# Splitting w1's conversion into three slices, moving g's columns to their own PSUM bank, and holding back two later loads

## The chip, the cores and the metric

The kernel runs on one NeuronCore of one Trainium2 chip. The metric is the device time of one execution in microseconds (us), lower is better. The core's engines are called PE (TensorE, matrix products), DVE (VectorE), ACT (ScalarE), POOL (GpSimd) and SP (SyncE, which here only issues DMAs). "PEld" stands for PE's weight loads.

## What is computed

x is float32 of 8 x 4224 x 192. A causal convolution of seven taps runs along the sequence, with one softmax-normalised set of taps for each of 8 heads of 24 channels. Its result goes through a layer norm (with gain g), two matrix products with a ReLU between them, and a residual sum:

```python
w = np.exp(weight - np.max(weight, axis=-1, keepdims=True))
w = w / (np.sum(w, axis=-1, keepdims=True) + 1e-09)          # weight: 8 heads x 7 taps
x_unf = x_pad[:, idx, :].reshape(B, S, K, H, group)          # K = 7, H = 8, group = 24
x = np.einsum('hk,bskhg->bshg', w, x_unf).reshape(B, S, D)   # D = 192
mu = np.mean(x, axis=-1, keepdims=True)
var = np.mean((x - mu) ** 2, axis=-1, keepdims=True)
xn = (x - mu) / np.sqrt(var + 1e-06) * g_ln
ch = np.maximum(xn @ w_ch1, 0.0) @ w_ch2                     # 192x768 and 768x192
return (x + ch).astype(np.float32)
```

The two matrices arrive as float64. The kernel reads them as pairs of 32-bit words and builds float32 from the bits itself.

## The kernel before

**Groups.** The sequence is cut into groups of rows, each laid over 128 partitions: group 0 has 6 rows for each partition, group 1 has 8 (the rows left over, from all eight batches), group 2 has 10, and from group 3 on there are 16. The main loop (L967) goes through the groups: `up` or `up_mixed` makes the hidden layer on PE, `down` or `down_fast` brings it back to 192 channels, and between them the convolution, transpose and statistics of the next groups are worked on by DVE and ACT. The schedule is manual: every engine runs its instructions in the order in which the program writes them, and the framework puts in the semaphores.

**The start**, which is all that the change touches, has these pieces.

- *Small inputs* (L195 to L209). ACT issues three small DMAs: the weights of the taps (L197) and g in two pieces (L199, L200). PE spreads the weights over all partitions with a matmul against a row of ones (L203), and turns g into two columns with two matmuls against ones (L205). All three write the bank `spread`. L268 to L277 make the normalised `taps` on DVE, with the exponential on ACT (L272); `gs` is the copy of g's columns (L273).
- *Loads on SP* (L211 to L224): w1's first 128 rows in one transfer into `raw1[:, 0:2]` (L211), the other 64 rows as two transfers into `raw1[:, 2]` (L215), group 0's x (`load_x(0)`: partitions 16 to 127, then 1 to 15 (L164), then the first (L171)), group 1's x (`load_x(1)`: eight transfers of 16 partitions each, L139), and w2's words (L221).
- *Words to float32*. `split_words` (L231) issues three DVE instructions (L233, L235, L239) and two on ACT (L234, L242); `join_words` (L244) issues three on DVE (L247, L250, L258 with g, or L256 without). w1 goes through in two pieces, of 768 columns (`words_a`) and of 384 (`words_b`), into `w1f`; w2 in one of 1152 columns later (L952 to L955).
- *Tap matrices*. For heads 5, 6 and 7 (`PE_HEADS`) the convolution of group 0 runs on PE, against diagonal matrices that hold the taps. `tap_matrices` (L324) writes those of heads 5 and 6 on ACT (L327), three taps before and four after w1's first split. POOL builds those of head 7 (L319).
- *Warm-up*. `keep_warm(20)` (L943) issues 20 matmuls of constants that POOL filled (`less`, L306, and `copy`); each shows as two passes, so as 40 instructions at L376.
- *Group 0's convolution.* `first_tap` (ACT, L397) starts `y` for heads 0 to 4, `conv` (DVE, L422) adds the other six taps, `transpose` (DVE, L433) prepares `yt` for PE.
- *`centre_w1`* (L340) takes the column means out of w1 on PE. In order: the mean's products over `w1f`'s slices 0 and 1 (L343), the convolution of one head (L334), the products over slice 2 (L346) with their copies (L347), a second head, then for slices 0, 2 and 1 the products L358 and L363 into four banks each and four copies on ACT (L368) into `w1`. The third head comes after slice 0.
- *The main stream*. `up(0)` (L544) takes sets of four PSUM banks, multiplies `yt` with `w1` (L538), and each set is evicted by ACT with a ReLU (L528).

PSUM has eight banks. `take_bank` (L119) deals them out in turn, `take_set` (L124) rounds up to the next multiple of four.

## Time and profile before

| what | value |
|---|---|
| median of 3 runs | 964.65 us (964.38 to 965.06) |
| profiled execution | 964.9 us, of which the span is 963.2 us |
| PE busy | 951.7 us (99%) |
| DVE busy | 894.1 us (93%) |
| ACT busy | 683.9 us (71%) |
| POOL busy | 252.8 us (26%) |
| DMA | 166.69 MB, mean 173 GB/s |
| first L538 (main stream on PE) | 27.31 us after the span's start |

The span is the time from the first to the last record of the profiled execution; all times of single instructions count from its start. Busy times overlap between engines. A busy PE is not a PE at its peak. In a line of a timeline the first number is the start, the second how long it lasts; then come engine, program line, operation, what it writes and reads, and in square brackets how long the engine idled before it and what ended that idle time. A chain of waits goes back from the last instruction, always to what released it.

### The profile page before, as it was taken

Reading aid. Unit: us, or ns where it says so; the run is one execution under the profiler, and the core shown is the slowest. Engines: PE = TensorE matmul, PEld = TensorE weight load, DVE = VectorE, ACT = ScalarE, POOL = GpSimd, SP = SyncE. Lnnn points to the kernel's source line nnn. Section 1 sums busy time; section 2 is a strip of 40 time slices with the busy share of each in tenths; the row PEclk is TensorE's granted clock in tenths of the full one; section 3 lists DMA queues with packets and bytes.
Section 4 is the critical chain, followed back from the end, with each engine's and each line's share of the span. In section 5 each row is a group of like instructions: output and inputs, shape, how many; then the busy total and the mean of one; then the engine's idle time right before and its main releaser. Section 6 shows DMA issues by size and latency. Waiting matters only on the chain.

```text
span 963.2 us, 38407 instructions
## 1 busy us (share of the span) xinstructions
PE 951.7 (99%) x17280; PEld 717.3 (74%) x17280; DVE 894.1 (93%) x1503; ACT 683.9 (71%) x1101; POOL 252.8 (26%) x386
## 2 busy tenths in 40 slices
PE   7999999999999999999999999999999999999997
PEld 6886586776858677686968778695867868586787
DVE  6999998999999999999999999999999899999757
ACT  5724669587787959687795968779695877867451
POOL 2004411612125131432116131341215221161400
PEclk9999999999999999999999999999999999999999
DMA  9343787769788796969788796978779696777241
GB/s 191 107 125 133 156 213 183 192 125 282 142 241 162 201 201 125 275 134 256 144 232 165 170 246 121 276 139 237 158 180 228 118 282 135 180 136 127 52 85 68
DMA packets 26234, 166.69 MB, mean 173 GB/s; under 512 B 3157, under 2 KB 4054, under 8 KB 18263
## 3 DMA queue, kind: packets, MB, share of 16 engines
q0 software_dynamic: 19552, 100.93, 54.4%
q1 hardware_dynamic: 6512, 63.31, 18.0%
q8 instruction: 135, 2.21, 0.9%
q14 instruction: 29, 0.24, 0.1%
q10 hardware_dynamic: 6, 0.00, 0.0%
HBM read 38.93 MB, written 50.33 MB: 93 GB/s over the span
## 4 chain that ended last, share of the span: by engine, by line
PE 95%; DMA 2%; POOL 1%; ACT 1%; DVE 1%; issue 0%; ACTq 0%; POOLq 0%; DVEq 0%
PE ps L538 46%; PE ps L816 41%; PE ps L763 6%; DMA room<-parts_cs 1%; PE ps L376 1%; DMA room<-in_moe_g_ln_dram 1%; PE ps L334 1%; DVE room L783 0%; DMA out_dram<-y 0%; ACT room L634 0%; DMA room<-room 0%; ACT room L647 0%; POOL d L465 0%; PE ps L358 0%; POOL room L601 0%
## 5 line engine op out<-in xcount | busy, mean ns | idle before, releaser
L422 DVE SCALAR_TENSOR_TENSOR y<-xg,taps,y 128x384 f32<-128x384 f32 (+3 forms) x734 | 367.2, 577 | 0.2
L538 PE MATMUL ps<-yt,w 32*128 32x256 f32 (+2 forms) x4104 | 236.2, 379 | 0.2 <-ACT room L528 0.2
L816 PE MATMUL ps<-room,w2sums 128*32 128x256 f32 (+1 forms) x4320 | 236.2, 375 | 0.1
L634 ACT COPY room<-ps 128x1024 f32<-128x1024 f32 (+1 forms) x135 | 175.0, 1297 | 78.2 <-PE ps L538 77.9
L538 PEld LDWEIGHTS ps<-yt,w 32*128 32x128 f32 x4104 | 204.7, 185 | 26.6 <-issue 9.3
L816 PEld LDWEIGHTS ps<-room,w2sums 128*32 128x32 f32 x4320 | 137.6, 110 | 93.4 <-ACT room L647 5.5
L816 PE MATMUL ps<-room,w 128*32 128x256 f32 (+1 forms) x3240 | 180.7, 375 | 0.3 <-ACT room L647 0.2
L783 DVE TENSOR_TENSOR room<-room 128x1024 f32<-128x1024 f32 (+1 forms) x135 | 151.0, 1192 | 6.4 <-PE ps L816 6.4
L816 PEld LDWEIGHTS ps<-room,w 128*32 128x32 f32 x3240 | 103.8, 110 | 69.4 <-DVE room L640 5.0
L538 PE MATMUL ps<-ysums,w1sums 32*128 32x256 f32 x2160 | 124.9, 379 | 0.0
L538 PEld LDWEIGHTS ps<-ysums,w1sums 32*128 32x128 f32 x2160 | 108.7, 185 | 11.2 <-ACT room L634 3.6
L822 ACT COPY cs<-ps 128x256 f32<-128x256 f32 (+1 forms) x180 | 66.5, 372 | 42.6 <-PE ps L816 42.6
L647 ACT ACTIVATE room<-room 128x1024 f32<-128x1024 f32 (+1 forms) x74 | 90.7, 1250 | 7.3 <-DMA room<-parts_cs 7.1
L894 ACT ACTIVATE ot<-ot,r 128x192 f32<-128x192 f32 x232 | 94.0, 464 | 0.0
L901 POOL DMA_DIRECT2D out_dram<-ot x40 | 34.3, 1084 | 196.9 <-ACT ot L894 121.5
L397 ACT ACTIVATE y<-xg,taps 128x384 f32<-128x384 f32 (+3 forms) x141 | 72.6, 607 | 6.5 <-DVE st L453 6.5
L640 DVE TENSOR_TENSOR room<-room,ps 128x2048 f32<-128x2048 f32 x17 | 38.9, 2288 | 39.4 <-PE ps L538 37.1
L453 DVE BATCH_NORM_STATS2 st<-y 128x6 f32<-128x192 f32 x264 | 70.2, 344 | 0.0
L538 PE MATMUL ps<-yt,w1sums 32*128 32x256 f32 x1080 | 65.2, 380 | 0.0
L822 ACT COPY room<-ps 128x256 f32<-128x256 f32 (+1 forms) x90 | 33.6, 374 | 43.9 <-PE ps L816 35.0
L538 PE MATMUL ps<-ysums,w 32*128 32x256 f32 x1080 | 64.5, 376 | 0.0
L408 ACT ACTIVATE tb<-xg,taps 128x384 f32<-128x384 f32 x112 | 61.9, 636 | 0.0
(109 smaller groups left out, 888.2 us busy)
## 6 DMA issues: line engine op xcount, KB each, us to landing
xg<-in_x_dram SPq DMA_DIRECT2D x15, 2112.0 KB, 18.1
room<-room POOLq DMA_DIRECT2D x45, 512.0 KB, 5.3
out_dram<-ot POOLq DMA_DIRECT2D x29, 768.0 KB, 8.5
y<-tb POOLq DMA_DIRECT2D x28, 768.0 KB, 10.4
out_dram<-y SPq DMA_DIRECT2D x13, 1536.0 KB, 9.4
room<-parts_cs POOLq DMA_DIRECT2D x14, 1024.0 KB, 7.8
room<-parts_tb POOLq DMA_DIRECT2D x14, 1024.0 KB, 7.6
xg<-in_x_dram SPq DMA_DIRECT2D x1, 1536.0 KB
```

Source lines behind the costliest of these rows:

```text
L397: nc.scalar.mul(y[g][:, 0:n, cs], xg[g][:, 0:n, cs], taps[:, h, 0:1])
L408: nc.scalar.mul(tb[g][:, 0:n, cs], xg[g][:, 1 : 1 + n, cs], taps[:, h, 1:2])
L422: nc.vector.scalar_tensor_tensor(out=y[g][:, 0:n, cs], in0=t[:, k : k + n, cs], scalar=taps[:, h, k : k + 1], in1=y[g][:, 0:n, cs], op0=AL ...
L453: nc.vector.bn_stats(out=sums[g][:, j, :], in_=y[g][:, j, :])
L538: nc.tensor.matmul(banks[:, q, i * w : i * w + w], right[rows, c, P * i : P * i + P], left[rows, :, c, :], start=(first and c == 0 and i = ...
L634: nc.scalar.activation(dst, src, AF.Relu) if relu else nc.scalar.copy(dst, src)
L647: nc.scalar.activation(c, c, AF.Relu)
L763: nc.tensor.matmul(bank[C * q : C * q + C, 0:w], w2[:, f, C * c : C * c + C], left, start=(f == 0), stop=(f == NF - 1),)
L783: nc.vector.tensor_tensor(a[:, *dst, f], a[:, *left, f], a[:, *right, f], op=op)
L816: nc.tensor.matmul(dst[C * q : C * q + C, 0:w], right[:, f, C * c : C * c + C], left[:, f, q], start=(first and f == PAIR), stop=(f == PAI ...
L822: nc.scalar.copy(to[:, c], dst[:, 0:w].rearrange("p (j t) -> p j t", t=t))
L894: nc.scalar.mul(ots[g][:, j, :], ots[g][:, j, :], rstd[g][:, j : j + 1])
```

## The change

w1's first 128 rows come in two transfers, one for each slice of 384 columns. w1 is converted in three slices of 384 columns, the split of one slice ahead of the join of the slice before. g's two matmuls go to a bank of their own, after six of the warm-up matmuls; four more come after them, and `keep_warm(20)` goes. `gs` is copied on ACT after the first slice's split. `tap_matrices` writes the seven matrices of one head at a time, head 5 after the join of slice 0 and head 6 after that of slice 1. The heads on PE go in the order 7, 5, 6. The loads of w2's words and of group 1's x are issued after a one-element memset of w2's tile on DVE, which comes after the join of slice 1; w2's words are now ahead of group 1's x.

```diff
-    for r in range(2):
-        nc.tensor.matmul(
-            spread[:, H * K + r : H * K + r + 1], g_row[:, P * r : P * r + P], ones[:, 0:1],
-            start=True, stop=True,
+    raw_taps = spread[:, 0 : H * K].rearrange("p (h k) -> p h k", k=K)
+
+    for s in range(2):
+        nc.sync.dma_start(
+            out=raw1[:, s].rearrange("p f w -> p (f w)"),
+            in_=w1_words[0:P, 2 * FH * s : 2 * FH * (s + 1)],
         )
-    raw_taps = spread[:, 0 : H * K].rearrange("p (h k) -> p h k", k=K)
-
-    nc.sync.dma_start(
-        out=raw1[:, 0:2].rearrange("p s f w -> p (s f w)"), in_=w1_words[0:P, :]
-    )
     for r in range(2):
         nc.sync.dma_start(
             out=raw1[Q * r : Q * r + Q, 2, :, :].rearrange("p f w -> p (f w)"),
             in_=w1_words[P:D, 2 * FH * r : 2 * FH * (r + 1)],
         )
     load_x(0)
-    load_x(1)
-    nc.sync.dma_start(
-        out=raw2.rearrange("p (c d) w -> p c (d w)", d=D),
-        in_=w2_words.rearrange("(c p) d -> p c d", p=P),
-    )
...
-    raw1a = raw1[:, 0:2].rearrange("p s f w -> p (s f) w")
-    raw1b = raw1[:, 2]
...
     nc.scalar.activation(taps, taps, AF.Exp)
-    nc.scalar.copy(gs, spread[:, H * K : H * K + 2])
...
-    words_a = (raw1a, carve(2 * FH, I32), carve(2 * FH, I32))
-    words_b = (raw1b, carve(FH, I32), carve(FH, I32))
+    words_1 = [(raw1[:, s], carve(FH, I32), carve(FH, I32)) for s in range(3)]
...
-    def tap_matrices(ks):
-        for k in ks:
-            for i, h in enumerate(PE_HEADS[:-1]):
-                nc.scalar.mul(diag[:, i, k, :], unit, taps[:, h, k : k + 1])
+    def tap_matrices(h):
+        for k in range(K):
+            nc.scalar.mul(diag[:, h - PE_HEADS[0], k, :], unit, taps[:, h, k : k + 1])
...
-        conv_on_pe(PE_HEADS[0])
+        conv_on_pe(PE_HEADS[2])
         for r in range(2):
             nc.tensor.matmul(pm[r], share[1 + r], w1f[:, 2, :], start=False, stop=True)
             nc.scalar.copy(mean[:, FH * r : FH * r + FH], pm[r])
-        conv_on_pe(PE_HEADS[1])
+        conv_on_pe(PE_HEADS[0])
...
             if s == 0:
-                conv_on_pe(PE_HEADS[2])
+                conv_on_pe(PE_HEADS[1])
...
-    tap_matrices(range(3))
-    split_words(*words_a)
-    tap_matrices(range(3, K))
-    join_words(w1f[:, 0:2].rearrange("p s f -> p (s f)"), *words_a, ga)
-    split_words(*words_b)
-    join_words(w1f[:, 2], *words_b, gb)
+    keep_warm(6)
+    g_cols = take_bank()
+    for r in range(2):
+        nc.tensor.matmul(
+            g_cols[:, r : r + 1], g_row[:, P * r : P * r + P], ones[:, 0:1], start=True, stop=True
+        )
+    keep_warm(4)
+    for s in range(3):
+        split_words(*words_1[s])
+        if s == 0:
+            nc.scalar.copy(gs, g_cols[:, 0:2])
+        else:
+            join_words(w1f[:, s - 1], *words_1[s - 1], ga)
+            tap_matrices(PE_HEADS[s - 1])
+    nc.vector.memset(raw2[0:1, 0:1, :], 0)
+    nc.sync.dma_start(
+        out=raw2.rearrange("p (c d) w -> p c (d w)", d=D),
+        in_=w2_words.rearrange("(c p) d -> p c d", p=P),
+    )
+    load_x(1)
+    join_words(w1f[:, 2], *words_1[2], gb)
...
-    keep_warm(20)
     first_tap(0, heads=(0, PE_HEADS[0]))
```

## The prediction

> **What bounds the kernel now.** I read the page first: its chain of what ended last says which engine sets the end.

> ```profile
> PE 95%; DMA 2%; POOL 1%; ACT 1%; DVE 1%; issue 0%; ACTq 0%; POOLq 0%; DVEq 0%
> ```

> After the start the matrix engine (PE) never rests, so a microsecond is won only by letting its main stream begin earlier. The diff touches nothing after about 27 us. Next comes the chain of waits of the first 40 us (start, length, what):

> ```profile
> 1.57 5.42 DMA room<-in_moe_g_ln_dram
> ...
> 7.03 0.58 PE ps L205 x2
> 7.62 7.52 PE ps L376 x40
> 15.13 1.43 PE ps L343 x4
> ...
> 26.24 1.41 ACT w L368 x4
> ...
> 31.75 0.81 ACT room L528
> ...
> 32.60 7.41 PE ps L538 x166
> ```

> The 40 L376 passes (the warm-up) fill a wait and do no work. L343 needs w1f, so the timelines of VectorE (DVE) and ScalarE (ACT) tell what it really waited for:

> ```profile
> 7.65 0.22 DVE L268 TENSOR_REDUCE wmax<-ps 128x8 f32<-128x56 f32 x1 [6.59 <-PE ps L205]
> ...
> 16.44 1.62 ACT L397 ACTIVATE y<-xg,taps 128x144 f32<-128x144 f32 x5
> ...
> 17.17 0.62 DVE L258 SCALAR_TENSOR_TENSOR room<-room,gs 128x384 f32<-128x384 f32 x1
> 17.70 6.78 DVE L422 SCALAR_TENSOR_TENSOR y<-xg,taps,y 128x144 f32<-128x144 f32 x24
> ...
> 30.59 1.26 ACT L242 ACTIVATE spare<-spare,low 128x1152 int32<-128x1152 int32 x1 [0.15 <-DVE spare L239]
> 31.75 0.80 ACT L528 ACTIVATE room<-ps 128x768 f32<-128x768 f32 x1
> ```

> VectorE sits 6.59 us until g's matmuls (L205) end, although the taps need only the weights' matmul, over at 2.78 (2.14+0.64). Then it works without a hole worth naming: w1 until 17.79, the convolution from 17.70, the second transpose until 28.45, w2's words from 28.38. At 30.59 the ACT step of w2 waits for it, and that step stands ahead of the first eviction (L528), for which PE waits at 32.56. So **VectorE's start sets PE's steady start**, from 32.60 on.

> Two details weigh below. The warm-up alone, in two stretches (7.5 to 13.4 and 13.6 to 15.2; durations are min/median/max):

> ```profile
> L376 PEld LDWEIGHTS ps<-room x28: 289/333/337, 7.5 to 13.3; 128*128 128x128 f32 x28
> ...
> L376 PEld LDWEIGHTS ps<-room x12: 192/192/240, 13.5 to 14.8; 128*128 128x128 f32 x12
> ```

> ```profile
> 28.10:28.50 0.40, 0.40 (x7) 1.00 0.00 0
> 28.50:28.90 0.40, 0.40 (x16) 1.00 1.06 426
> ```

> PE begins up(0) at 27.31 but runs freely from about 28.3 only: L368 copies eight banks of w1 from 26.22 on (8 in 3.16 us, 0.38 apart), and the first matmul into each bank waits for its copy.

> [...] L235 took 1.34 us over 768 columns beside POOL's L319, but 0.75 over 1152 alone.

> **The change part by part.** Times are the span's.

> *g in its own bank.* wmax goes from 7.65 to 2.82. The small steps from wmax to the end of taps took 1.70 us (7.65 to 9.35), 0.04 of it waiting for gs: taps are done at about 4.5, 4.85 earlier.

> *w1 in three slices.* In before the large transfer, issued at 0.80, lands 6.0 later (6.8), the two small ones at 8.2 and about 8.9 (6.7 to 7.1 after issue). The bytes are the same: I estimate slice 0 at 4.7 (half of the large one), slice 1 at 6.8, slice 2 at 8.9. VectorE's cost of a 384-column slice is read from the second half of before: split 0.94 (14.87 to 15.81), join 1.75. Three slices are 8.1 us against 8.5 now (9.26 to 17.79). Split 0 runs from 4.7 and meets POOL's L319 (5.4 to 6.6): up to 1.2 us lost, as L235 lost about 0.8. Then split 1, join 0, split 2, join 1, join 2 follow. Join 0 needs gs, so it ends near 9.5; join 1 near 12.1; join 2, which waits for ACT, near 14.1 (17.79 now).

> *g's columns on PE.* keep_warm(6) can start when POOL filled `less` (4.83): 12 passes of 0.21 plus 0.2 for the first end at 7.6. g has landed by 7.0. Two L205 of 0.5 to 0.58 end at 8.65, and gs is copied at 8.7.

> *ACT's queue, the new bound.* In order behind gs: L234 and L242 of slice 1, seven tap matrices, L234 and L242 of slice 2, seven tap matrices, then first_tap. Durations 0.52, 0.62 and 0.30 (8 in 2.43): 2x1.14 + 14x0.30 = 6.5, less 0.1 of overlap at each of the four longer ones, 6.1 us. first_tap starts at 14.8 (16.44 now), its first head ends at 15.2. VectorE, free at 14.1, waits for it, so the convolution starts at 15.2 against 17.70: **2.5 us earlier**. All 24 conv steps, both transposes, w2's words, L242 and L528 follow at the same distances. If gs were earlier, join 2 (14.1) would be the bound, worth at most 1.1 us more.

> *PE's path.* L343 of the second half waits for join 1 (12.1), head 7's convolution follows at 12.8 to 13.1 (16.40 now), gain 3.3 or more. All later pieces have the same durations. The order of heads puts first the one that POOL built, so no tap matrix is late. But two more banks are taken (19 to 21), and up(0) takes its set by fours: its four banks become the 4th to 7th of the eight w1 copies; now they are the 2nd to 5th. Two copies of 0.37 make 0.74 us lost, net gain 2.6. It comes in just ahead of ACT's 2.5.

> *x of group 0.* Its landing is at 14.9 and 15.7 now (12.4 after 2.47, 12.6 after 3.06), while group 1's eight transfers crowd it from 6.79. Without them 2.3 MB at the 295 GB/s that the windows show between 8 and 10 us take 8 us from 1.8, plus up to 3 for engines that lag: 12.5 to 13.2. It is wanted at 12.8 by PE, at 14.8 by ACT.

> *Held back.* The memset of one element costs VectorE at most 0.17 us (L201's length) ahead of join 2. Queued behind it on SP: w2's issue and eight loads of x, 12 to 22 us, then store_y(0), wanted at 25.1. w2 took 9.7 us to land: 22, wanted at 25.9. x of group 1 lands near 26, wanted at 30. These hide; if SP came 4 us later, store_y would be next.

> *Sum.* The profiled execution took 964.9 us, span 963.2, so 1.7 lie around it. 963.2 - 2.5 = 960.7, plus 1.7 is 962.4. The runs' median is 0.25 lower than the profiled run, so 964.65 - 2.5 = **962.15**.

> **Rivals.**

> 1. *The clock rises too late.* Warm-up passes fall from 40 to 20, with the one-column g matmuls between. If PE counts as busy throughout, from 4.85 to about 11.7 (2.75 + 1.05 + 1.7 of warm-up and g, then half an L343 at half rate, 1.3), that is 6.8 us, above the 6.4 seen. If the g matmuls don't count, [...] gain near 0.3, **964.3**. For: the first stretch in before (7.03 to 10) wasn't enough. Against: it too began with a g matmul.
> 2. *x of group 0 stays late.* If its last 15 rows, all in 15 neighbouring partitions, are what was slow, it lands near 15.2, first_tap starts 1.2 earlier than now: **963.4**. Against: moved bytes fall from 295 to 40 GB/s at 11 us just when group 1's transfers arrive.
> 3. *Slower: the clock again[...].* [...] Lost 4 to 5 us against 2.9 ahead: **966.2**. It is slower once the rise comes after about 18.

> **How the numbers follow.** Forecast 0.60 (own range 961.2 to 963.0: [...] join 2 as bound below); rival 1 0.22; rival 2 0.10; rival 3 0.08. Down to 961.2 and up to 965.2 leaves out little below and rival 3 with the upper end of rival 1 above. 0.2% is 1.9 us, about what a measurement of this kernel tells from no change. Below 962.7 lie most of the forecast's cases and a few of rival 2: 0.54. Above 966.6 lies part of rival 3: 0.05. The rest, 0.41, is within.

> **What will show it.** wmax near 2.8; gs near 8.7; ACT without a hole from there to first_tap at 14.8; the convolution at 15.2; L346 pieces at 1.3 us (2.6 would be the half clock); L538 free from 25.7; the first L528 near 29.3. I am wrong if L334 or L397 waits for x, if PE's passes are still 0.21 after 12 us, or if PE pauses later than 40 us where it doesn't now.

## The result and the profile after

| | before | after |
|---|---|---|
| median of 14 runs, us | 965.18 (964.38 to 967.23) | 962.87 (961.66 to 964.26) |
| profiled execution, us | 964.9 | 964.26 |
| its span, us | 963.2 | 962.5 |

The ratio is 0.9975, with a 95% interval of 0.9967 to 0.9984: 2.3 us gained, a quarter of a per cent. The forecast of 962.15 (from a first median of 964.65) meant a ratio of 0.9974; the range, 961.2 to 965.2, holds the result. The two spans alone would show only 0.7 us, since the profiled execution of after was the longest of its 14. So the gain is read from the runs, and the place of it from the first 30 us of the trace.

The chain of what ended last, of after:

```profile
PE 90%; POOL 3%; DMA 3%; DVE 2%; ACT 1%; issue 1%; POOLq 0%; ACTq 0%; DVEq 0%
```

PE still sets the end. The chain of waits of the first 40 us of after (start, length, what):

```profile
5.07 2.93 PE ps L363 x12
8.00 0.95 PE ps L368 x4
8.98 0.17 ACT gs L375
...
12.37 1.63 PE ps L330 x2
13.99 1.72 PE ps L321 x14
...
23.67 1.62 ACT w L355 x4
...
25.33 13.39 PE ps L540 x288
```

The 5.42 us of transfer that headed this chain in before are gone: behind POOL's fills, left out here, it now runs through warm-up, g, `gs`, VectorE's work on w1 (in the lines left out) and then PE to the up products, which begin at 25.33 (27.31 in before) and run on without a break through the first eviction. The timeline of after shows how the other engines get there (start, length, engine and line, then the wait in brackets):

```profile
2.82 0.22 DVE L258 TENSOR_REDUCE wmax<-ps 128x8 f32<-128x56 f32 x1 [1.76 <-PE ps L203]
...
8.98 0.16 ACT L375 COPY gs<-ps 128x2 f32<-128x2 f32 x1 [2.70 <-PE ps L368]
...
13.65 0.62 DVE L250 SCALAR_TENSOR_TENSOR room<-room,gs 128x384 f32<-128x384 f32 x1
...
14.98 1.62 ACT L399 ACTIVATE y<-xg,taps 128x144 f32<-128x144 f32 x5
15.47 6.81 DVE L424 SCALAR_TENSOR_TENSOR y<-xg,taps,y 128x144 f32<-128x144 f32 x24 [1.19 <-ACT y L399]
...
29.55 0.79 ACT L530 ACTIVATE room<-ps 128x768 f32<-128x768 f32 x1
```

VectorE begins the taps at 2.82 (7.65 in before), because their wait for g's matmuls is gone. It has finished w1 by 14.27, waits 1.19 us for ACT's `first_tap`, and starts the convolution 2.23 us earlier than before (17.70). The first eviction comes 2.20 earlier (31.75 in before). The 1.19 us in brackets are the next bound: ACT's queue.

Behind the first eviction the profiles differ by less than the 2.6 us over which the 14 runs of after spread, and this is taken as accident here. Span less start of the first eviction is 931.45 us in before, 932.9 in after, and from 931.5 to 933.0 over the ten further profiles below, whose instructions are the same from there on. Much of what after lost there shows in ACT's waits for DMA in `room<-parts_cs`; the costliest groups, of before and of after:

```profile
L647 ACT ACTIVATE room<-room 128x1024 f32<-128x1024 f32 (+1 forms) x74 | 90.7, 1250 | 7.3 <-DMA room<-parts_cs 7.1
```

```profile
L649 ACT ACTIVATE room<-room 128x1024 f32<-128x1024 f32 (+1 forms) x74 | 90.7, 1250 | 10.6 <-DMA room<-parts_cs 10.6
```

The same 74 instructions of the same length waited 3.5 us more. A single span can't weigh an edit of 2 us here.

### The profile page after: what moved, and what is told of

Read it like the earlier page. It is cut to its first block, busy times and chain, and to the rows that moved or that the text cites. A ratio compares the mean times of both kernels' runs of the same rounds, so it can differ in the third digit from the quotient of the medians.

```text
span 962.5 us, 38377 instructions
## 1 busy us (share of the span) xinstructions
PE 951.6 (99%) x17260; PEld 721.3 (75%) x17260; DVE 894.6 (93%) x1510; ACT 683.4 (71%) x1103; POOL 251.8 (26%) x386
## 4 chain that ended last, share of the span: by engine, by line
PE 90%; POOL 3%; DMA 3%; DVE 2%; ACT 1%; issue 1%; POOLq 0%; ACTq 0%; DVEq 0%
PE ps L540 42%; PE ps L818 41%; PE ps L765 6%; DMA room<-room 2%; DVE room L785 1%; DMA room<-parts_cs 1%; ACT room L636 1%; PE ps L321 1%; POOL room L603 1%; POOL d L467 0%; POOL r L490 0%; POOL d L486 0%; POOL d L485 0%; PE ps L363 0%; ACT room L649 0%
## 5 line engine op out<-in xcount | busy, mean ns | idle before, releaser
L540 PE MATMUL ps<-yt,w 32*128 32x256 f32 (+2 forms) x4104 | 235.9, 379 | 0.4 <-ACT w L355 0.4
L540 PEld LDWEIGHTS ps<-yt,w 32*128 32x128 f32 x4104 | 204.4, 185 | 27.1 <-issue 9.1
L818 PEld LDWEIGHTS ps<-room,w2sums 128*32 128x32 f32 x4320 | 141.8, 110 | 89.6 <-ACT room L649 5.2
L818 PEld LDWEIGHTS ps<-room,w 128*32 128x32 f32 x3240 | 106.5, 110 | 67.2 <-DVE room L642 5.0
L540 PE MATMUL ps<-ysums,w1sums 32*128 32x256 f32 x2160 | 125.0, 379 | 0.0
L540 PEld LDWEIGHTS ps<-ysums,w1sums 32*128 32x128 f32 x2160 | 108.9, 185 | 11.0 <-ACT room L636 3.6
L540 PE MATMUL ps<-yt,w1sums 32*128 32x256 f32 x1080 | 65.3, 380 | 0.3 <-ACT room L636 0.2
L540 PE MATMUL ps<-ysums,w 32*128 32x256 f32 x1080 | 64.6, 376 | 0.0
```

The source lines that it names most:

```text
L540: nc.tensor.matmul(banks[:, q, i * w : i * w + w], right[rows, c, P * i : P * i + P], left[rows, :, c, :], start=(first and c == 0 and i = ...
L818: nc.tensor.matmul(dst[C * q : C * q + C, 0:w], right[:, f, C * c : C * c + C], left[:, f, q], start=(first and f == PAIR), stop=(f == PAI ...
```

## The experiments

Each kernel was timed beside the kernel before on the same chip; a ratio is to that. "First eviction" is the start of the first L530 (the line number shifts a little from kernel to kernel), "copies" the start of the eight copies of w1's last parts (L355 of after), "convolution" that of VectorE's 24 steps. The labels in brackets are those by which the recorded expectations name each other. The last three columns are of one profile each.

| kernel | median, us (runs) | ratio and interval | convolution | copies | first eviction |
|---|---|---|---|---|---|
| before | 965.18 (14) | | 17.70 | 26.22 | 31.75 |
| after | 962.87 (14) | 0.9975 [0.9967, 0.9984] | 15.47 | 23.65 | 29.55 |
| bank alone (e1) | 964.94 (13) | 0.9993 [0.9985, 1.0002] | 15.78 | 24.70 | 30.78 |
| two pieces (e2) | 962.35 (8) | 0.9972 [0.9962, 0.9982] | 15.01 | 23.00 | 29.09 |
| not held, x first (e3) | 964.03 (13) | 0.9992 [0.9984, 1.0001] | 15.47 | 23.84 | 31.38 |
| not held, w2 first (e9) | 962.98 (15) | 0.9979 [0.9971, 0.9986] | 15.48 | 24.01 | 29.56 |
| bank and order (e10) | 963.96 (22) | 0.9989 [0.9982, 0.9996] | 15.33 | 24.32 | 29.50 |
| one bank less (e4) | 963.32 (21) | 0.9983 [0.9977, 0.9990] | 15.46 | 22.93 | 29.55 |
| no warm-up (e6) | 963.03 (17) | 0.9979 [0.9971, 0.9986] | 13.50 | 23.71 | 28.89 |
| early warm-up, head 6 on POOL (e8) | 964.10 (14) | 0.9990 [0.9980, 1.0001] | 14.20 | 25.32 | 30.51 |
| warm throughout (e11) | 961.15 (5) | 0.9959 [0.9946, 0.9971] | 13.79 | 22.50 | 27.88 |
| changed again (e12) | 962.97 (8) | 0.9976 [0.9965, 0.9986] | 15.06 | 22.54 | 29.15 |

**The bank alone.** On the kernel before, only g's two matmuls move:

```diff
+    g_cols = take_bank()
     for r in range(2):
         nc.tensor.matmul(
-            spread[:, H * K + r : H * K + r + 1], ...
+            g_cols[:, r : r + 1], ...
-    nc.scalar.copy(gs, spread[:, H * K : H * K + 2])
+    nc.scalar.copy(gs, g_cols[:, 0:2])
```

> The kernel before with one edit: g's two columns go to a PSUM bank of their own. Theory (freeing the taps from g lets VectorE start early, but x of group 0, crowded by group 1's loads, lands near 15.7 us and then holds first_tap): taps done near 4.5 us, w1's first split at its landing (6.8 us), first_tap at 15.9, the convolution at 16.3 instead of 17.7, first eviction of up(0) at 30.6 instead of 31.75, total 1.1 us less than before. Rival 'the bank is the whole change': convolution at 15.5, total 2.3 less. Rival 'the bank brings nothing, other waits take over': total within 0.3.

The convolution came 1.92 us earlier, yet the median moved by nothing that can be told. VectorE's timeline of this kernel:

```profile
15.78 6.78 DVE L422 SCALAR_TENSOR_TENSOR y<-xg,taps,y 128x144 f32<-128x144 f32 x24
...
27.36 0.76 DVE L233 TENSOR_SCALAR spare<-raw 128x1152 uint32<-128x1152 uint32 x1 [0.83 <-DMA raw<-in_moe_w_ch_dram]
```

A new wait stands behind the convolution, for w2's words. VectorE reaches them 1.85 us sooner, at 26.53 (28.38 in before), and they land later than in before. Their transfer (L221) was issued at 15.91 (16.71 in before) and took:

```profile
DMA to landing us min/median/max: 11.4/11.4/11.4
```

In before it took 9.7 us and landed at 26.4, which would just have done here. Why it took longer is not shown. About half of the gain goes there in this profile. The theory's own wait did not come: `first_tap` started at 14.76, not at 15.9, since group 0's x landed 11.6 us after its issue instead of 12.5.

**Two pieces instead of three slices.** On the changed kernel, w1's first 128 rows come by one transfer and are converted as one piece of 768 columns and one of 384; all else stays.

```diff
-    for s in range(2):
-        nc.sync.dma_start(out=raw1[:, s]..., in_=w1_words[0:P, 2 * FH * s : ...])
+    nc.sync.dma_start(out=raw1[:, 0:2]..., in_=w1_words[0:P, :])
-    for s in range(3):
-        split_words(*words_1[s])
...
+    split_words(*words_a)
+    nc.scalar.copy(gs, g_cols[:, 0:2])
+    tap_matrices(PE_HEADS[0])
+    join_words(w1f[:, 0:2]..., *words_a, ga)
+    split_words(*words_b)
+    tap_matrices(PE_HEADS[1])
```

> The changed kernel with w1 back in two pieces (768 and 384 columns, one transfer for the first), all else of the change kept. Theory (ACT's queue from the copy of gs to first_tap is the bound, so slices are hidden): first_tap near 15.1 us, convolution near 15.5, first eviction near 29.6, total as the changed kernel within 0.3 us. Rival 'the slices bring the gain': w1 is joined a microsecond or more later, convolution at 16.3 or later, total 0.8 or more above the changed kernel.

It keeps the whole gain (0.9972). VectorE still waits for ACT by the same amount ahead of the convolution, so what the slices save on VectorE can't be seen. It even starts 0.46 us earlier than in the changed kernel, since `gs` comes 0.20 earlier (8.78) and ACT's queue behind it takes 5.74 us instead of 6.00:

```profile
15.01 1.23 DVE L423 SCALAR_TENSOR_TENSOR y<-xg,taps,y 128x144 f32<-128x144 f32 x4 [1.19 <-ACT y L398]
```

**Hold and order apart.** Two kernels without the memset and its wait. In the first, group 1's x goes out right behind group 0's and w2's words after it, as in the kernel before; in the second w2's words go ahead of group 1's x, as in the changed kernel, but at once.

```diff
-    nc.vector.memset(raw2[0:1, 0:1, :], 0)
...
     load_x(0)
+    load_x(1)
+    nc.sync.dma_start(out=raw2..., in_=w2_words...)
```

In the second kernel the last two lines change places.

> The changed kernel without the hold: the loads of group 1's x and of w2's words are issued right after group 0's x, as before. Theory: group 0's x lands at 15.2 to 15.7 us again (12.4 to 12.6 after its issue), PE's first head waits for it to 15.8 (13.8 with the hold), so PE's path is 2.0 later and the total is 1.5 to 2.0 above the changed kernel, about that of before. Rival 'the hold brings nothing': x is wanted by ACT only at 15.0, total within 0.5 of the changed kernel.

> The changed kernel without the memset and the hold, but with the changed order: group 0's x, then w2's words, then group 1's x, all issued at once. Theory from e3 (what the held-back part is worth is w2's place ahead of group 1's x; e3 lost 1.7 us waiting for w2's words at 26.2 us): w2 lands before 20 us, convolution at 15.5, first eviction of up(0) at 29.6, total within 0.3 us of the changed kernel. Rival 'the hold itself matters, w2's 768 short packets crowd group 0's x': PE's first head at 15 us or later (13.8 with the hold), convolution after 16, total 0.8 or more above the changed kernel.

The timeline of the first, x ahead of w2 (SPq is SP issuing transfers):

```profile
4.37 10.27 SPq L139 DMA_DIRECT2D xg<-in_x_dram  x8
...
15.13 0.41 SPq L218 DMA_DIRECT2D raw<-in_moe_w_ch_dram  x1
...
27.96 0.76 DVE L230 TENSOR_SCALAR spare<-raw 128x1152 uint32<-128x1152 uint32 x1 [1.71 <-DMA raw<-in_moe_w_ch_dram]
```

The eight issues of x by themselves (nanoseconds, min/median/max):

```profile
L139 SPq DMA_DIRECT2D xg<-in_x_dram x8: 310/314/419, 4.4 to 14.2; - x8
```

And of the second, w2 ahead of x:

```profile
4.37 0.41 SPq L217 DMA_DIRECT2D raw<-in_moe_w_ch_dram  x1
...
6.10 13.59 SPq L139 DMA_DIRECT2D xg<-in_x_dram  x8
...
26.18 0.72 DVE L230 TENSOR_SCALAR spare<-raw 128x1152 uint32<-128x1152 uint32 x1
```

Eight loads of x occupy SP for 10.27 us, though each is issued in 0.31 to 0.42: SP stands between them, longest from 8.03 to 12.72, just when group 0's x has landed (2.94 + 9.8). So w2's one transfer goes out at 15.13, lands at 27.96, and VectorE stands 1.71 us. Issued ahead, at 4.37, it is there when wanted. The second kernel has the time of the changed one, so the hold brings nothing, and without the order most of the gain is lost. The first kernel's expectation had the loss right in kind but from another wait: it let PE wait for group 0's x to 15.8, and PE's first head began at 13.95. Its x landed as early as in the changed kernel, which the prediction had credited to the hold. From the transfers of group 0's x, without hold:

```profile
DMA to landing us min/median/max: 9.8/9.8/9.8
```

In the changed kernel it is the same 9.8. It was 10.3 to 12.6 us in the three kernels that have the start of before, and 8.0 to 10.1 in the others; which part of the change sets it was not found.

**Bank and order.** The two parts that count, on the kernel before: the edit of "bank alone", and w2's transfer moved ahead of `load_x(1)`.

> The kernel before with two edits alone: g's bank (as in e1) and w2's words ahead of group 1's x. Theory: the convolution at 15.8 to 16.3 us as in e1, no wait for w2's words at 26, so the first eviction comes at 29.8 to 30.3 instead of 30.8, total 1.5 to 1.9 below before, most of the change's 2.3. Rival 'order brings nothing without the slices': first eviction at 30.8, total 0.6 below before as e1.

The wait for w2's words is gone (the split of w2 starts at 26.01 without a wait) and the first eviction of this profile stands where the changed kernel has it. The median says about half of the gain, 1.0 us, less than the 1.5 to 1.9 expected. What the other half needs was not separated: besides slices and hold, which bring nothing by themselves, the changed kernel has other places for the warm-up, the copy of `gs` and the tap matrices, and another order of the heads. The order of the loads alone, without g's bank, was not run. Here all 40 warm-up passes stand between g and w1, so PE's path has less room: the copies start 0.7 us later than in the changed kernel. One candidate, as an estimate: a pass takes 0.21 us before the clock's rise (28 in 5.8 us in before) and about 0.11 after it (13 in 1.45 us here), so each microsecond by which the clock rises later than in this profile (10.58) adds about 0.5 us to the 40 passes, on the path that sets the first eviction here. How often it does is not on record.

**One bank less.** On the changed kernel both batches of warm-up share a bank, so up(0) gets a set of banks that is filled earlier.

```diff
+    idle = take_bank()
     def keep_warm(times):
-        idle = take_bank()
```

> The changed kernel, but both warm-up batches share one PSUM bank, so that up(0)'s set of banks falls on the first four of the eight w1 copies (in the changed kernel the fourth to seventh). Theory: PE runs up(0) freely from about 25.3 us instead of 26.5, then stands at the first eviction, which VectorE's chain sets: third hidden row tile of up(0) at 30.4 as now, total within 0.3 of the changed kernel. Rival 'the banks are the bound': the third row tile and the total 0.7 or more earlier.

PE is free in up(0) at 24.6 instead of 26.5, part of it from a clock that rose 1.5 us earlier in this profile (12.33 instead of 13.84), and nothing comes of it. Its timeline shows why:

```profile
24.03 1.82 PE L541 MATMUL ps<-yt,w 32*128 32x192 f32 x24
26.30 3.21 PE L541 MATMUL ps<-yt,w 32*128 32x192 f32 x72 [0.44 <-DVE yt L436]
30.39 3.82 PE L541 MATMUL ps<-yt,w 32*128 32x192 f32 x84 [0.88 <-ACT room L531]
```

PE waits 0.44 us for the second transpose and 0.88 for the first eviction, which starts at 29.55 as before.

**No warm-up.** Both `keep_warm` calls of the changed kernel are removed.

> The changed kernel without its ten warm-up matmuls; g's two matmuls then run as soon as g lands. Theory: gs at 7.5 us (9.0 with them), first_tap at 13.5 and the convolution at 14.3, but [...] L343-like passes are 0.64 us and the head's convolution 0.24 us a pass[...]; up(0) runs freely 1.5 to 3 us later than in the changed kernel and the total is 0.5 to 2 above it. Rival 'the clock is hidden behind VectorE and ACT': total 0.5 or more below the changed kernel, because gs comes earlier.

Neither came: the time is that of the changed kernel. Without the 12 passes ahead of them g's matmuls are over early, `gs` is copied at 6.19 (8.98), and VectorE's convolution starts 2 us earlier. But PE's own timeline is at half rate:

```profile
11.70 1.65 PE L330 MATMUL ps<-room 128*128 128x384 f32 x2 [0.81 <-DVE raw L377]
13.14 2.63 PE L321 MATMUL ps<-xg,room 128*128 128x144 f32 x14
```

The head's convolution takes 2.63 us instead of 1.9, and PE reaches the copies at 23.71, no earlier than with the warm-up. So the table holds two paths to the first eviction. Where VectorE is late, it comes 14.05 to 14.09 after the convolution's start (before, after, two pieces, not held with w2 first, one bank less, warm throughout, changed again). Where PE is late, it comes 5.18 to 5.19 after the start of the copies (here, bank and order, early warm-up), because ACT has to end them first. The later one decides, and in the changed kernel they are 0.7 us apart: 15.47 + 14.08 = 29.55 against 23.65 + 5.18 = 28.83.

**Early warm-up, head 6 on POOL.** The warm-up reads a tile that VectorE fills at the very start, and POOL builds head 6's tap matrices, so that ACT has seven less.

```diff
+    filled = carve(2 * P, F32)
+    nc.vector.memset(filled, 1.0)
+    idle = take_bank()
+    keep_warm(2)
     spread = take_bank()
...
-    keep_warm(6)
+    keep_warm(9)
...
+    nc.gpsimd.affine_select(out=diag[:, H - 2 - PE_HEADS[0]], ...)
...
-            tap_matrices(PE_HEADS[s - 1])
+            if s == 1:
+                tap_matrices(PE_HEADS[0])
```

> Three edits on the changed kernel: the warm-up runs from about 1.3 us on a tile that VectorE fills (11 matmuls ahead of g's, then 4), in one PSUM bank; head 6's tap matrices are built by POOL and not by ACT. Theory (ACT's queue is the bound, then the join of slice 2; x of group 0 at 13.2): first_tap near 13.2, convolution near 14.0 instead of 15.5, PE's first head near 13.2 at full clock, first eviction near 28.1, total 1.2 to 1.5 below the changed kernel. Rival [...]: the join of slice 2 after 15, gain under 0.4.

This missed. The wait for ACT is gone and the convolution starts at 14.20, but PE's path is now the late one:

```profile
3.13 3.93 PE L208 MATMUL ps<-room 128*128 128x128 f32 x18
...
7.53 1.16 PE L208 MATMUL ps<-room 128*128 128x128 f32 x8
...
10.30 1.62 PE L345 MATMUL ps<-room 128*128 128x384 f32 x2 [1.62 <-DVE room L261]
12.73 1.65 PE L345 MATMUL ps<-room 128*128 128x384 f32 x2 [0.81 <-DVE raw L389]
...
14.17 3.21 PE L336 MATMUL ps<-xg,room 128*128 128x144 f32 x14
```

The last 8 warm-up passes take 0.15 us each against 0.22 of the first 18: the clock had doubled, at 6.64. At 10.30 two L345 passes take 1.62 us (0.91 for the same two at full rate, in "changed again"): it was lost again, and the head's convolution took 3.21. Here the granted clock shows it, in windows of this kernel (time, length, busy time of PE, PEld, DVE, ACT and POOL, then PEclk, DMA share and GB/s):

```profile
10.00:10.20 0.20, 0.00 (x0) 0.00 (x0) 0.20 (x2) 0.20 (x2) 0.00 (x0) 0.64 0.21 46
10.20:10.40 0.20, 0.10 (x1) 0.13 (x1) 0.20 (x2) 0.20 (x2) 0.00 (x0) 0.50 1.01 138
...
16.80:17.00 0.20, 0.20 (x3) 0.20 (x3) 0.20 (x2) 0.00 (x0) 0.00 (x0) 0.80 1.05 353
17.00:17.20 0.20, 0.20 (x4) 0.20 (x3) 0.20 (x2) 0.00 (x0) 0.00 (x0) 1.00 0.91 346
```

It fell at 10.06 (0.64 is the mean of 0.06 us at 1.00 and 0.14 at 0.50) and came back at 16.88. PE had been idle from 8.7 to 10.3.

**Warm throughout, and the changed kernel again.** The same early tile, head 6 back on ACT, and warm-up passes spread so that PE has no hole: two ahead of the weights' matmul, five ahead of g, six behind it, three between the two halves of w1's first product.

```diff
-    keep_warm(6)
+    keep_warm(5)
...
-    keep_warm(4)
+    keep_warm(6)
...
             nc.tensor.matmul(pm[r], share[0], w1f[:, r, :], start=True, stop=False)
+            if r == 0:
+                keep_warm(3)
```

> The changed kernel with PE kept busy from 1.4 us to the head's convolution: warm-up matmuls on a tile that VectorE fills, 2 ahead of the weights' matmul, 5 ahead of g's, 6 after them and 3 between the two halves of the mean's product (e8's clock rose at 6.5 us and was lost again in PE's pauses of 8.4 to 12.7), in one PSUM bank; ACT keeps head 6's matrices. Theory (the clock, and g's place on PE, are what the changed kernel still loses): gs near 6.5 us, first_tap near 13.1, convolution near 13.5, PE's first head near 13.2 with passes of 0.12 us throughout, first eviction near 28.4 instead of 29.55, total 0.8 to 1.2 below the changed kernel and narrower in spread. Rival 'the clock is no limit by then': first eviction at 28.9 as in e6 without warm-up, total within 0.3 of the changed kernel.

> The changed kernel as it is, beside e11 on the same chip. Theory (its clock rises at a moment that differs from run to run): total 962.9 as before, the first head's passes at 0.24 or 0.12 us depending on the execution; first_tap and convolution at 15.0 and 15.5 whatever the clock. Rival 'the clock's rise is fixed by the program': rise at 13.8 us again.

It is the fastest, and by more than the 0.8 to 1.2 expected: 961.15, 4.0 below before and 1.8 below the changed kernel on the same chip, with its 5 runs (960.80 to 961.93) all below the 8 of the changed kernel (962.25 to 963.94). PE's timeline:

```profile
6.50 2.93 PE L208 MATMUL ps<-room 128*128 128x128 f32 x12
9.51 1.00 PE L341 MATMUL ps<-room 128*128 128x384 f32 x2
10.34 0.83 PE L208 MATMUL ps<-room 128*128 128x128 f32 x6
11.94 0.91 PE L341 MATMUL ps<-room 128*128 128x384 f32 x2 [0.77 <-DVE raw L386]
12.69 1.88 PE L332 MATMUL ps<-xg,room 128*128 128x144 f32 x14
```

The clock rises at 9.75 and stays (PEclk 1.00 on to 40 us). Both paths moved: convolution 13.79, copies 22.50, and the first eviction 27.88. The edit also takes g's matmuls earlier (`gs` 7.32 instead of 8.98), so it changes both; that it has one bank less gained nothing by itself. Neither of the two is seen to do it alone: "no warm-up" had g still earlier with a slow PE, and its runs gained nothing, and the changed kernel's second profile has PE as fast as here with g late, and its first eviction came at 29.15, only 0.4 us before that of the first profile. That second comparison is of single profiles.

The changed kernel run again shows that its clock is not fixed by the program. PE's timeline of after, and then of the same program in its second profile:

```profile
5.07 2.93 PE L363 MATMUL ps<-room 128*128 128x128 f32 x12 [2.29 <-POOL room L294]
7.93 1.01 PE L368 MATMUL ps<-room 1*128 1x1 f32 x4
8.87 2.08 PE L363 MATMUL ps<-room 128*128 128x128 f32 x8
10.74 3.25 PE L330 MATMUL ps<-room 128*128 128x384 f32 x4
13.81 1.90 PE L321 MATMUL ps<-xg,room 128*128 128x144 f32 x14
```

```profile
7.93 0.61 PE L368 MATMUL ps<-room 1*128 1x1 f32 x4
8.47 1.16 PE L363 MATMUL ps<-room 128*128 128x128 f32 x8
9.47 0.89 PE L330 MATMUL ps<-room 128*128 128x384 f32 x2
11.97 0.91 PE L330 MATMUL ps<-room 128*128 128x384 f32 x2 [1.61 <-DVE raw L379]
12.72 1.88 PE L321 MATMUL ps<-xg,room 128*128 128x144 f32 x14
```

Both are busy from 5.07. In the first the eight passes at 8.87 take 2.08 us and full rate begins at 13.84; in the second they take 1.16 and it began at 7.99. With the faster clock g's matmuls ended sooner (0.61 us instead of 1.01), so `gs` and the convolution came 0.4 us earlier there, against the expectation's "whatever the clock".

## Why the prediction was right, and where it was not

- *What bounds the kernel: right.* With nothing but g's bank moved, VectorE began at once and the convolution came 1.92 us earlier.
- *The bank step: right.* `wmax` starts at 2.82 as said; taps end at 4.6 (4.5 said).
- *Slices: right in time, idle in effect.* Slice 0 is split from 4.53 and join 2 ends at 14.27 (14.1 said). Beside POOL's L307 (5.74 to 6.72) VectorE lost about 0.4 us of the 1.2 allowed: an L225 took 0.70 us there and 0.35 elsewhere. Two pieces do as well, as the step itself implied by finding ACT later than join 2.
- *g on PE and ACT's queue: right.* `gs` at 8.98 (8.7 said), since the warm-up began 0.2 us late, behind a POOL fill of 0.40. The queue behind it took 6.0 us (6.1 said), the convolution starts at 15.47 (15.2), and the gain is 2.23 instead of 2.5. The 1.19 us that VectorE waits is the term that the step named.
- *PE's path: a term mis-sized.* Said was 12.8 to 13.1 for the head's convolution at full rate, a gain of 3.3, less 0.74 for the banks, net 2.6. It began at 13.81: gain 2.6, because the second product of w1, from 12.37, still ran at half rate (0.8 us a pass against 0.45), as rival 1 had it. Passes at half rate after 12 us were one of the prediction's own signs of being wrong; it came true, and cost nothing that the time shows, because VectorE's path was as late. Less the banks, PE is free at 26.5 instead of 28.3, net 1.8. The banks' term itself holds: the copies gain 2.57, PE's free run 1.80, so 0.77. In after the windows of L540 show it (the count of passes stands in brackets):

```profile
25.70:26.10 0.40, 0.40 (x5) 1.00 1.40 202
26.10:26.50 0.40, 0.40 (x7) 1.00 0.58 85
...
29.30:29.70 0.40, 0.40 (x20) 1.00 0.93 392
```

  Five and seven passes in 0.4 us where 20 are possible. PE needs just the time that the eviction leaves it, and so this costs nothing yet; "one bank less" took it away and gained nothing.
- *Rival 1, the clock: partly real.* How late the rise would come if g's matmuls don't count as busy was the author's estimate. In the profiles with a warm-up it came anywhere from 6.64 ("early warm-up") to about 14.6 ("not held, w2 first", whose first head took 2.25 us instead of 1.9), and in one program at 7.99 and 13.84. In after PE was busy without a break from 5.07 to 12.23, 1.01 us of it with g's matmuls (from 7.93), and the clock did not rise until 13.84. In the second profile it rose at 7.99, after 2.92 us of warm-up passes and next to none of g's. That g's matmuls did not count, as the rival feared, would fit the late rise of the first, but it is an estimate from these two profiles, and no run tests it alone. The loss that the rival drew from it did not come: at half rate the first half of w1's product kept PE at work until 12.23, the second began at 12.37, and by 13.84 the clock had risen.
- *x of group 0: right in time, wrong in cause.* 12.5 to 13.2 was said, and its two large transfers landed 9.8 us after issue, at 12.7 and 13.4. But the step gave that to the absence of group 1's transfers, and without the hold it was 9.8 as well.
- *Held back: it hides, as said, but the step that failed is what it left out.* It priced the new order of w2 and x as a cost to be hidden. The order is what makes the gain possible: with x first, w2's words come at 27.4 to 28.0, when VectorE, now 2 us earlier, wants them at 26.2 to 26.5. Before had 2 us of slack there (landing at 26.4, wanted at 28.4). The earlier VectorE uses that up, and the waits of 0.83 and 1.71 us are nearly what the transfer landed later than in before, which stays unexplained. The prediction did not ask when this transfer would land with the old order. That its number held is luck in this respect: the same working would have given 2.5 us to the kernel with x first, which measured 0.9992, some 0.8 us.
- *The sum: right*, 2.5 said for 2.3. The first eviction came 0.27 less early than said through ACT's queue and a `gs` 0.3 late; the 0.8 missing on PE's path (1.8 for 2.6) fell where VectorE's path was as late.

## What to carry to other kernels

When a stall at the head of an engine's queue goes, list for every later input of that engine when it lands and when it will now be wanted; here a transfer with 2 us of slack would have taken most of a 2.2 us gain, and its place in the issuing queue was worth more than its hold. Work out the two or three paths that meet at the point that matters as sums (here convolution + 14.08 and copies + 5.18) and move them together, since moving one alone gained nothing twice. Where a whole run jitters by as much as the edit is worth, compare medians of many runs for the size and marks of the first stretch for the place.

## What the runs showed of the hardware

- The doubled matrix clock was lost again in "early warm-up". It rose at 6.64, fell at 10.06 and rose again at 16.88. Of the 3.41 us from the rise to the fall PE was busy for 2.04, 0.60 of it with g's matmuls, and idle from 8.7 on. Of the next 3.41 us it was busy for 2.34, and the clock stayed at 0.50; of the 3.41 us before the second rise it was busy for all.
- How much idle time loses the clock does not come out. PE stood for 1.62 us ahead of 10.30 in "early warm-up", and the clock fell; it stood for 1.61 us ahead of 11.97 in "changed again", and the two L330 passes after that took 0.91 us, full rate. At the end of after PE's last pass was over at 957.36, and PEclk prints 1.00 up to the span's end at 962.47. In before it was over at 958.06, and PEclk is 0.88 from 962.40 to 962.50, so the fall came at about 962.5.
- The moment of the first rise is not set by the passes ahead of it alone. After and "changed again" are one program, with the same twelve passes from 5.07 to 7.93, and the clock rose at 13.84 in the one and at 7.99 in the other. Whether g's one-column matmuls count for it is not shown; the estimate above rests on these two profiles.
- PEclk shows the fall as 0.50, but printed 1.00 through the half rate stretches ahead of a first rise, such as that from 8.87 in after, where eight passes took 2.08 us against 1.16 in "changed again". The time of a pass is the safer sign.
- SP stood between issues. The eight loads of x took 0.31 to 0.43 us each to issue in before, but kept SP for 9.72 us there, 9.2 to 13.6 in the kernels without a hold and 6.0 to 7.1 in those with one. In before one of SP's pauses ended at 14.89, when the first large transfer of group 0's x had landed (2.47 + 12.4); in "not held, x first" one ended at 12.72 (landing at 2.94 + 9.8). The transfer of w2's words behind the eight loads went out at 16.71 and at 15.13. What limits SP is not shown.
- VectorE lost time beside POOL's building of tap matrices (128x896). In after one of the three instructions of a 384-column split took 0.70 us in place of 0.35 while POOL built head 7's, and in "early warm-up" the same instruction took 1.13 while POOL built head 6's (6.52 to 7.61).
